# A transformer block on one core: the order of the first hundred microseconds, and the later layernorms on GpSimd

## The chip, the cores and the metric

The kernel runs as one program on one core of a Trainium2 chip. The core has five engines that each work through their own queue in order and wait for each other by semaphores: TensorE (PE, matrix products, results to PSUM), VectorE (DVE), ScalarE (ACT, activation functions), GpSimd (POOL) and SyncE (SP, which here issues all DMAs). The metric is the device time of one execution in microseconds; less is better.

## The reference

The reference is a pre-layernorm attention block followed by a gated bilinear block, both with a residual. Sequence 2048, model width 640, 32 heads of width 20, inner width 1728, everything in bfloat16:

```python
def _layernorm(x, axis=-1, eps=1e-5):
    m = jnp.mean(x, axis=axis, keepdims=True)
    v = jnp.var(x, axis=axis, keepdims=True)
    return (x - m) / jnp.sqrt(v + eps)

# attention
qkv = (x @ wqkv).reshape(B, S, 3, H, Dh).transpose(2, 0, 3, 1, 4)
scores = jnp.einsum("bhqd,bhkd->bhqk", q, k) * (Dh ** -0.5)
o = jnp.einsum("bhqk,bhkd->bhqd", softmax(scores), v)
attention = o.transpose(0, 2, 1, 3).reshape(B, S, D) @ wo
# gated bilinear block
h = (x @ w_gate) * (x @ w_up)
bilinear = h @ w_down

h  = x + attention(_layernorm(x))
h2 = h + bilinear(_layernorm(h))
```

## The kernel before

**Attention.** The 32 heads form 8 groups of four; the 2048 rows form 16 row tiles of 128 and four chunks of 512 (NB = 4, TPB = 4 row tiles in a chunk). Scores are computed transposed: for a key tile and a head, TensorE multiplies a piece of kT (32 x 128, head width padded to 32) with 512 columns of the queries. Three such products fill a PSUM tile `sc` of 128 x 1536 (three banks); there are two `sc` tiles. ScalarE takes the exponential of one in a single instruction into an SBUF tile `E` (L388); six E tiles rotate. TensorE then multiplies the E pieces with the padded V (with a column of ones, for the sums) into the one `acc` bank (AV, L474). One `sc` tile with its exponential is called a tile here, numbered from 0; there are 683. The first ones belong to the first 512 queries: for each key chunk, groups 0 to 3 in turn, five and a third tiles for each chunk and group.

**All other work is cut in between.** The eighth PSUM bank, `mi`, is a single buffer that every other product goes through: transposes of the normalised x (`job_T`, L223, five products, copied to lnT), projections to Q and K (`job_proj`, L241, five products of 512 columns, cast to qa or kT), V (`job_V`, L251, five products of 320 columns, cast to vx), and later the output projection and the bilinear block. A job cannot begin before DVE has emptied the bank of the job before it.

**The order** is written by the kernel's own planner, while it is built. `jobs` is a queue of generators that are filled in once (L584 to L627). For each tile i the main loop (L885) emits the scores and the exponential (`emit_S`), a piece of about 640 ns of the job at hand (`go_on`), AV products of earlier tiles (`emit_AV`: those up to i - 2, at most four at a time for 512 columns), and one step of the layernorms (`step_aux`). `emit_S` and `emit_AV` call `ensure` for what they need (Q, K or V), which runs the queue on until that job is done, in one go. So where a projection is not ready in the queue when its tile comes, all of it is emitted ahead of that tile's scores.

**The head.** The first chunk of x arrives in four pieces. PE does 40 products of the identity into `mi` (WARM, L518). Row tiles 0 and 1, and then 2 and 3, are normalised as pairs (`bn`, `rstd_act`, `apply1`), the square root on ACT. Each row tile is transposed (`first_T`), into `mi` for even and into `acc` for odd row tiles; ACT copies the even ones out, DVE the odd ones. `pad_half` spreads the weights to 32 columns a head: c 0, 1, 2 on ACT and 3, 4 on GpSimd for the first half of the heads, and all five on GpSimd for the second half. When all four are there, Q and K of group 0 are projected for both pairs (L553, twenty products of 256 columns, into the two `sc` tiles), ACT loads the table of Exp, and K and Q are cast by ACT and DVE.

**The later layernorms.** `gen_ln(ch)` makes the layernorm of chunks 1 to 3 in eleven steps: batch statistics of four row tiles, three steps of `rstd_steps`, and four of `apply1`. `rstd_steps` rounds mean and variance to bfloat16 and finds the square root by an integer start and three Newton steps, all on 128 x 4 values; all of this was on DVE. Chunks 2 and 3 of x are loaded into a buffer that an earlier chunk has to leave (two `xs` buffers). The steps of the second layernorms in the bilinear part use the same `rstd_steps`.

In the queue before, chunk 0 has its four V jobs and then Q and K of groups 1 to 3. A later chunk begins with its four transposes one after the other, then the load of x for two chunks later, K of group 0, V, and K of groups 1 to 3.

## Time and profile before

| | us |
|---|---|
| median of three runs | 1007.26 (1007.16 to 1008.3) |
| the profiled execution | 1010.34 |
| its span, first to last instruction | 1008.5 |
| first exponential (L388) starts | 17.92 |
| ACT busy in the span | 940.2 |
| PE busy in the span | 892.4 |
| DVE busy in the span | 322.6 |
| GpSimd busy in the span | 8.2 |
| five wp copies of GpSimd (second half of the heads) | 15.11 to 18.48 |
| load of the last chunk of x issued | 45.80 |

The span is the time between the first and the last instruction of the program, the profiled execution's time is what the device reports for it. In the profile's lines "E<-sc" is what is written and read, "x5" counts merged instructions, and a bracket holds the idle time of the engine before it and who ended it. The two numbers that begin a line of the timeline are the start and the length in microseconds. A line of the windows names the stretch, its length, the busy time of PE, PEld, DVE, ACT and POOL, the granted clock of TensorE, the DMA engines' busy share and GB/s. An engine that is busy for most of the span is not yet the bound; the chain that ended last tells which one is waited for.

### The profile page before, as it was taken

To read this page: it belongs to the slowest core of one execution; us is meant where nothing else is said; L and a number is where in the kernel's file an instruction comes from. 1 tells how busy PE (TensorE), PEld (TensorE's weight loads), DVE (VectorE), ACT (ScalarE), POOL (GpSimd) and SP (SyncE) were. 2 spreads that over 40 slices of the span, in tenths; PEclk is the share of its full clock that TensorE was granted. 3 is DMA by queue.
4 is the path that set the end of the run, shared out by engine and by line. 5 is a ranking of instruction groups with operands and counts; after the bars stand their busy time and mean duration, and the time that the engine had idled before them with its cause. 6 is when DMAs were issued, how large, how long until landed. Compare 5 with 4: busy or idle time off the path is not lost.

```text
span 1008.5 us, 17146 instructions
## 1 busy us (share of the span) xinstructions
PE 892.4 (88%) x7003; PEld 330.7 (33%) x7003; DVE 322.6 (32%) x804; ACT 940.2 (93%) x719; POOL 8.2 (1%) x62
## 2 busy tenths in 40 slices
PE   7889999999798999977798999977898999989986
PEld 4233342222132223311132333411242333434454
DVE  7783343433044322100025332110044322243232
ACT  5789999999999999999999999999999999999931
POOL 3000000000000000000000000000000000000000
PEclk8889999999587999955577999965597999979989
DMA  6000010103421320100021220000502000202210
GB/s 177 27 1 1 1 35 12 45 12 112 151 72 36 89 58 19 33 12 12 7 59 38 71 78 12 32 19 11 152 2 64 13 13 12 74 12 60 79 34 16
DMA packets 67813, 44.40 MB, mean 44 GB/s; under 512 B 18504, under 2 KB 63404, under 8 KB 67728
## 3 DMA queue, kind: packets, MB, share of 16 engines
q1 hardware_dynamic: 67728, 43.23, 15.6%
q8 instruction: 57, 0.93, 0.4%
q14 instruction: 28, 0.23, 0.1%
HBM read 35.91 MB, written 7.30 MB: 43 GB/s over the span
## 4 chain that ended last, share of the span: by engine, by line
ACT 58%; PE 22%; issue 13%; DVE 6%; DMA 1%; ACTq 0%; DVEq 0%
ACT E L388 58%; PE sc L382 5%; PE mi L730 3%; PE acc L474 3%; PE f L730 2%; PE mi L667 2%; PE mi L254 2%; PE mi L244 1%; DVE st L160 1%; PE mi L226 1%; PE f L762 1%; PE mi L762 1%; DVE kT L213 0%; PE sc L553 0%; DVE hh L737 0%
## 5 line engine op out<-in xcount | busy, mean ns | idle before, releaser
L388 ACT ACTIVATE E<-sc 128x1536 bf16<-128x1536 f32 (+1 forms) x683 | 923.1, 1715 | 21.0 <-PE sc L382 19.9
L382 PE MATMUL sc<-qa,kT 32*128 32x512 bf16 x1536 | 234.7, 446 | 70.8 <-ACT E L388 66.4
L474 PE MATMUL acc<-E,vx 128*32 128x512 bf16 (+1 forms) x2432 | 234.3, 401 | 0.0
L382 PEld LDWEIGHTS <-kT 32*128 32x128 bf16 x2432 | 97.2, 93 | 303.7 <-issue 295.9
L474 PEld LDWEIGHTS <-vx 128*32 128x32 bf16 x2432 | 57.1, 95 | 162.9 <-issue 159.8
L244 PE MATMUL mi<-lnT,wp 128*128 128x512 bf16 x310 | 89.7, 389 | 2.9 <-DVE qa L213 1.2
L382 PE MATMUL sc<-qb,kT 32*128 32x256 bf16 (+1 forms) x896 | 72.9, 304 | 10.8 <-ACT E L388 9.4
L762 PE MATMUL mi<-wd,hh 128*128 128x320 bf16 x392 | 71.1, 304 | 0.1
L213 DVE CAST u<-mi 128x512 bf16<-128x512 f32 (+3 forms) x56 | 35.0, 624 | 92.6 <-PE mi L730 92.6
L737 DVE TENSOR_TENSOR hh<-mi,u 128x512 bf16<-128x512 f32 (+3 forms) x56 | 35.0, 625 | 86.3 <-PE mi L730 86.3
L486 DVE COPY asb<-acc 128x512 f32<-128x512 f32 (+1 forms) x33 | 19.8, 600 | 120.5 <-PE acc L474 120.5
L730 PE MATMUL mi<-ln2T,wu 128*128 128x512 bf16 (+2 forms) x200 | 55.9, 384 | 1.7 <-DMA wu<-in_B_w_up_dram 0.5
L730 PE MATMUL mi<-ln2T,wg 128*128 128x512 bf16 (+2 forms) x200 | 52.8, 367 | 0.7 <-DVE u L213 0.5
L762 PEld LDWEIGHTS <-hh 128*128 128x128 bf16 x448 | 36.8, 97 | 37.1 <-issue 27.1
L667 PE MATMUL mi<-wo,on 128*128 128x320 bf16 x224 | 42.1, 313 | 0.0
L765 DVE TENSOR_TENSOR xr<-mi,h 128x320 bf16<-128x320 f32 x28 | 13.8, 492 | 88.0 <-PE mi L762 88.0
L730 PE MATMUL mi<-ln2T,qa 128*128 128x512 bf16 (+3 forms) x160 | 34.2, 328 | 1.1 <-DVE u L213 0.5
L213 DVE CAST kT<-mi 128x512 bf16<-128x512 f32 x31 | 21.3, 689 | 41.7 <-PE mi L244 41.7
L244 PEld LDWEIGHTS <-wp 128*128 128x128 bf16 x310 | 21.3, 97 | 39.6 <-issue 31.2
L670 DVE TENSOR_TENSOR h<-mi,xr 128x320 f32<-128x320 f32 x28 | 13.8, 492 | 52.0 <-PE mi L667 51.6
L254 PE MATMUL mi<-wv,lnT 128*128 128x320 bf16 x160 | 27.0, 299 | 2.9 <-DVE vx L213 2.8
L412 DVE TENSOR_TENSOR on<-asb,bc 128x512 bf16<-128x512 f32 (+1 forms) x30 | 18.2, 605 | 32.8 <-DMA bc<-scr 32.8
(115 smaller groups left out, 400.8 us busy)
## 6 DMA issues: line engine op xcount, KB each, us to landing
bc<-scr SPq DMA_DIRECT2D x100, 64.0 KB
...
```

Source lines behind the costliest of these rows:

```text
L213: nc.vector.tensor_copy(dst, src)
L244: nc.tensor.matmul(ps[:], lhsT=wslice(m, g, c), rhs=lnT[:, c, ch * QB:(ch + 1) * QB], start=(c == 0), stop=(c == KT - 1))
L254: nc.tensor.matmul(ps[:, 0:HALF], lhsT=lnT[:, c, t * P:(t + 1) * P], rhs=wv[c][:, half * HALF:(half + 1) * HALF], start=(c == 0), stop=(c ...
L382: nc.tensor.matmul(sc[:, o:o + w], lhsT=kT[g][SLOT * j:SLOT * (j + 1), kt * P:(kt + 1) * P], rhs=q_of(g, b, c0, w)[SLOT * j:SLOT * (j + 1) ...
L388: nc.scalar.activation(e[:, 0:n], sc[:, 0:n], ACT.Exp, scale=SM_SCALE)
L412: nc.vector.tensor_tensor(On[b % 2][g][:, c0:c0 + w], asb[:, 0:w], bc[:, 0:w], ALU.mult)
L474: nc.tensor.matmul(acc["t"][SLOT * j:SLOT * (j + 1), 0:w], lhsT=vx[kt][:, VS * h:VS * h + SLOT], rhs=e, start=(kt == lo), stop=(kt == hi - 1))
L486: nc.vector.tensor_copy(asb[:, 0:w], acc["t"][:, 0:w])
L667: nc.tensor.matmul(ps[:, 0:HALF], lhsT=on[g][:, t * P:(t + 1) * P], rhs=wo[g][:, cs], start=(g == 0), stop=(g == NG - 1))
L730: nc.tensor.matmul(ps[0:M, 0:n], lhsT=st["w", fp][k][:, c, f2 * P:f2 * P + M], rhs=st["ln2T"][:, c, c0:c0 + n], start=(c == 0), stop=(c == ...
L737: nc.vector.tensor_tensor(st["hh"][2 * fp + f2][0:M, c0:c0 + n], ps[0:M, 0:n], hold["u"][0:M, 0:n], ALU.mult)
L762: nc.tensor.matmul(ps[:, 0:HALF], lhsT=st["hh"][f][0:K, t * P:(t + 1) * P], rhs=late["Wd"][f][0:K, cs], start=(f == 0), stop=(f == 2 * FP ...
```

## The change

In the head, row tile 0's and 1's part of Q and K of group 0 is projected right behind their transposes (`first_proj(0)`), and the other part behind the transposes of row tiles 2 and 3. The order within is changed to alternate K and Q for each of the five slices of the width. Products of the identity that nobody reads (`keep_busy`) stand ahead of it (52 in place of 40), between the first two transposes (2), behind them (6) and behind the first projection (4).

In the queue, chunk 0 begins with Q and K of group 1, ahead of V. The transposes of the next chunk are spread over the jobs of a chunk, one behind every second V and one behind the projections of groups 2 and 3. The load of x for the chunk after next comes behind them, followed by K of group 0 of the next chunk.

The layernorms of chunks 1 to 3 go to GpSimd, except for the batch statistics and the reciprocal, which stay on DVE. GpSimd takes one more operation in each Newton step; the integer shift is merged into the next operation on both engines. For the first 48 tiles two steps of the layernorms are emitted with each tile instead of one, and the layernorm of a chunk begins when its load has been emitted. For the first 10 tiles AV stays four tiles behind rather than two.

```diff
--- before.py
+++ after.py
@@ -48,7 +48,9 @@
 END = "end"
 BUDGET = 640
 START = 440
-WARM = 40
+WARM = 52
+LAG = 10
+EARLY = 48
 
 
 @with_exitstack
@@ -160,31 +162,35 @@
             nc.vector.bn_stats(st[:, h, :], halves[h] if halves else src[:, h * HALF:(h + 1) * HALF])
         nc.vector.bn_aggr(mv[:, k, :], st[:])
 
-    def rstd_steps(mv, n):
+    def rstd_steps(mv, n, ve_=None):
+        ve_ = ve_ or nc.vector
         mb = small.tile([P, n], BF16, name="mb")
-        nc.vector.tensor_copy(mb[:], mv[:, :, 0])
+        ve_.tensor_copy(mb[:], mv[:, :, 0])
         m32 = small.tile([P, n], F32, name="m32")
-        nc.vector.tensor_copy(m32[:], mb[:])
+        ve_.tensor_copy(m32[:], mb[:])
         vb = small.tile([P, n], BF16, name="vb")
-        nc.vector.tensor_copy(vb[:], mv[:, :, 1])
+        ve_.tensor_copy(vb[:], mv[:, :, 1])
         ve = small.tile([P, n], BF16, name="ve")
-        nc.vector.tensor_scalar_add(ve[:], vb[:], EPS_B)
+        ve_.tensor_scalar_add(ve[:], vb[:], EPS_B)
         v = small.tile([P, n], F32, name="v")
-        nc.vector.tensor_copy(v[:], ve[:])
+        ve_.tensor_copy(v[:], ve[:])
         yield
         y = small.tile([P, n], F32, name="y")
-        iy = small.tile([P, n], I32, name="iy")
-        nc.vector.tensor_scalar(iy[:], v[:].bitcast(I32), 1, None, ALU.arith_shift_right)
-        nc.vector.tensor_scalar(y[:].bitcast(I32), iy[:], -1.0, float(0x5F3759DF), ALU.mult, ALU.add)
+        ve_.tensor_scalar(y[:].bitcast(I32), v[:].bitcast(I32), -0.5, float(0x5F3759DF), ALU.mult, ALU.add)
         t = small.tile([P, n], F32, name="nt")
         for k in range(3):
-            nc.vector.tensor_tensor(t[:], y[:], y[:], ALU.mult)
-            nc.vector.scalar_tensor_tensor(t[:], t[:], -0.5, v[:], ALU.mult, ALU.mult)
-            nc.vector.scalar_tensor_tensor(y[:], t[:], 1.5, y[:], ALU.add, ALU.mult)
+            ve_.tensor_tensor(t[:], y[:], y[:], ALU.mult)
+            if ve_ is nc.gpsimd:
+                ve_.tensor_tensor(t[:], t[:], v[:], ALU.mult)
+                ve_.tensor_scalar(t[:], t[:], -0.5, 1.5, ALU.mult, ALU.add)
+                ve_.tensor_tensor(y[:], t[:], y[:], ALU.mult)
+            else:
+                ve_.scalar_tensor_tensor(t[:], t[:], -0.5, v[:], ALU.mult, ALU.mult)
+                ve_.scalar_tensor_tensor(y[:], t[:], 1.5, y[:], ALU.add, ALU.mult)
             if k == 0:
                 yield
         den = small.tile([P, n], BF16, name="den")
-        nc.vector.tensor_tensor(den[:], v[:], y[:], ALU.mult)
+        ve_.tensor_tensor(den[:], v[:], y[:], ALU.mult)
         r = small.tile([P, n], F32, name="rstd")
         nc.vector.reciprocal(r[:], den[:])
         yield (m32, r)
@@ -199,10 +205,11 @@
 
     lns = {}
 
-    def apply1(t, m32, r, k):
+    def apply1(t, m32, r, k, eng=None):
+        eng = eng or nc.vector
         x_t = xs[t // TPB][:, t % TPB, :]
-        nc.vector.tensor_scalar(x_t, x_t, m32[:, k:k + 1], None, ALU.subtract)
-        nc.vector.tensor_scalar(x_t, x_t, r[:, k:k + 1], None, ALU.mult)
+        eng.tensor_scalar(x_t, x_t, m32[:, k:k + 1], None, ALU.subtract)
+        eng.tensor_scalar(x_t, x_t, r[:, k:k + 1], None, ALU.mult)
         lns[t] = x_t
 
 
@@ -513,9 +520,11 @@
         nc.vector.reciprocal(r[:], den[:])
         return m32, r
 
-    idle = mip.tile([P, BANK], F32, name="mi", tag="mi")
-    for k in range(WARM):
-        nc.tensor.matmul(idle[:, 0:P], lhsT=ident[:], rhs=ident[:], start=True, stop=True)
+    def keep_busy(n):
+        idle = mip.tile([P, BANK], F32, name="mi", tag="mi")
+        for k in range(n):
+            nc.tensor.matmul(idle[:, 0:P], lhsT=ident[:], rhs=ident[:], start=True, stop=True)
+    keep_busy(WARM)
 
     def ln_bank(k):
         if k % 2:
@@ -525,6 +534,13 @@
     pair_mv = [small.tile([P, 2, 2], F32, name="mv") for _ in range(2)]
     pK = scp.tile([P, EW], F32, name="sc")
     pQ = scp.tile([P, EW], F32, name="sc")
+    def first_proj(pr):
+        for c in range(KT):
+            for m in (1, 0):
+                nc.tensor.matmul(
+                    (pQ, pK)[m][:, pr * HW:(pr + 1) * HW], lhsT=wslice(m, 0, c),
+                    rhs=lnT[:, c, pr * HW:(pr + 1) * HW], start=(c == 0), stop=(c == KT - 1))
+
     def first_T(t, eng, after=None):
         gen = job_T(lns[t], lnT[:, :, t * P:(t + 1) * P], eng, ln_bank(t), after)
         for _ in gen:
@@ -533,26 +549,23 @@
     for k in range(2):
         bn(pair_mv[0], k, xs[0][:, k, :])
     m32, r = rstd_act(pair_mv[0], 2, lambda: bn(pair_mv[1], 0, xs[0][:, 2, :]))
-    for c in (0, 1):
+    for c in (0, 1, 3, 4):
         pad_half(c, 0)
     for k in range(2):
         apply1(k, m32, r, k)
     first_T(0, "act")
     pad_half(2, 0)
+    keep_busy(2)
     first_T(1, "dve", lambda: bn(pair_mv[1], 1, xs[0][:, 3, :]))
-    for c in (3, 4):
-        pad_half(c, 0)
+    keep_busy(6)
+    first_proj(0)
+    keep_busy(4)
     m32, r = rstd_act(pair_mv[1], 2)
     for k in range(2):
         apply1(2 + k, m32, r, k)
     first_T(2, "act")
     first_T(3, "dve")
-    for pr in range(2):
-        for m in (1, 0):
-            for c in range(KT):
-                nc.tensor.matmul(
-                    (pQ, pK)[m][:, pr * HW:(pr + 1) * HW], lhsT=wslice(m, 0, c),
-                    rhs=lnT[:, c, pr * HW:(pr + 1) * HW], start=(c == 0), stop=(c == KT - 1))
+    first_proj(1)
     nc.scalar.activation(warm[:], ones[:], ACT.Exp)
     for c in range(KT):
         pad_half(c, 1)
@@ -564,13 +577,15 @@
     def gen_ln(ch):
         ts = range(ch * TPB, (ch + 1) * TPB)
         mv = small.tile([P, TPB, 2], F32, name="mv")
+        while ch not in xs:
+            yield
         for k in range(TPB):
             bn(mv, k, xs[ch][:, k, :])
             yield
-        for got in rstd_steps(mv, TPB):
+        for got in rstd_steps(mv, TPB, nc.gpsimd):
             yield
         for k, t in enumerate(ts):
-            apply1(t, *got, k)
+            apply1(t, *got, k, nc.gpsimd)
             done.add(("a", t))
             yield
 
@@ -582,18 +597,30 @@
         aux.append(gen_ln(ch))
 
     for ch in range(NB):
-        if ch:
-            for t in range(ch * TPB, (ch + 1) * TPB):
+        nxt = deque(range((ch + 1) * TPB, (ch + 2) * TPB) if ch + 1 < NB else [])
+
+        def one_T():
+            if nxt:
+                t = nxt.popleft()
                 add(("T", t), T_of(t))
-            if ch + 2 < NB:
-                do(("x", ch + 2), lambda ch=ch: load_x(ch + 2))
-            add(("k", 0, ch), job_proj(1, 0, ch))
+        if ch == 0:
+            add(("q", 0, 1), job_proj(0, 1, 0))
+            add(("k", 1, 0), job_proj(1, 1, 0))
         for t in range(ch * TPB, (ch + 1) * TPB):
             add(("v", t, 0), job_V(t, 0))
+            if t % 2:
+                one_T()
         for g in range(1, G1):
-            if ch == 0:
+            if ch == 0 and g > 1:
                 add(("q", 0, g), job_proj(0, g, 0))
-            add(("k", g, ch), job_proj(1, g, ch))
+            if ch or g > 1:
+                add(("k", g, ch), job_proj(1, g, ch))
+            if g > 1:
+                one_T()
+        if ch + 1 < NB:
+            if ch + 3 < NB:
+                do(("x", ch + 3), lambda ch=ch: load_x(ch + 3))
+            add(("k", 0, ch + 1), job_proj(1, 0, ch + 1))
     for g in range(G1, NG):
         add(("q", 0, g), job_proj(0, g, 0))
         for ch in range(NB):
@@ -891,8 +918,10 @@
                 ensure(("spill", g))
             load_res()
         used = go_on(BUDGET)
-        emit_AV(i - 2 if i < n_tiles else i)
+        emit_AV(i if i >= n_tiles else i - 2 if i >= LAG else i - 4)
         step_aux()
+        if i < EARLY:
+            step_aux()
         run_events(i)
         if b_seen < NB - 1 and normed(str(b_seen), range(NG)):
             add_tail(b_seen, list(range(TPB)))
```

## The prediction

> **What bounds the kernel now.** I read the page first: busy shares, the slices and the chain that ended last.
>
> ```profile
> PE 892.4 (88%) x7003; PEld 330.7 (33%) x7003; DVE 322.6 (32%) x804; ACT 940.2 (93%) x719; POOL 8.2 (1%) x62
> ...
> PEclk8889999999587999955577999965597999979989
> ...
> ACT 58%; PE 22%; issue 13%; DVE 6%; DMA 1%; ACTq 0%; DVEq 0%
> ```
>
> ACT is busy for 93% of the span and carries the chain: the 683 exps of L388, 1.33 us from one to the next, set the time. The change touches only the first hundred microseconds, so the second view is the busy time of each engine by stretch, cut at the first exp (17.92), at the end of the last gap of the head (74.45) and at the last exp.
>
> ```profile
> 0.00:17.92 17.92, 11.30 (x84) 8.88 (x85) 11.59 (x38) 7.33 (x12) 7.65 (x62) 0.81 0.84 241
> 17.92:74.45 56.53, 48.70 (x332) 16.98 (x332) 44.76 (x145) 47.47 (x35) 0.56 (x1) 0.88 0.05 15
> 74.45:959.40 884.95, 796.50 (x6313) 278.67 (x6312) 250.50 (x575) 874.50 (x648) 0.00 (x0) 0.87 0.16 43
> ```
>
> The columns are PE, PEld, DVE, ACT and POOL busy, then the granted clock. ACT idles 9.1 us between 17.92 and 74.45 and only 10.5 us in the 885 us behind. What the head wins or loses in exp starts moves the end by as much. Third, the timeline of ACT alone, where the bracket is the idle time before an exp:
>
> ```profile
> 28.09 6.89 ACT L388 ACTIVATE E<-sc 128x1536 bf16<-128x1536 f32 x5 [3.25 <-PE sc L382]
> ...
> 42.97 1.45 ACT L388 ACTIVATE E<-sc 128x1536 bf16<-128x1536 f32 x1 [0.84 <-PE sc L382]
> ...
> 48.90 4.52 ACT L388 ACTIVATE E<-sc 128x1536 bf16<-128x1536 f32 x3 [1.03 <-PE sc L382]
> ...
> 68.48 1.45 ACT L388 ACTIVATE E<-sc 128x1536 bf16<-128x1536 f32 x1 [1.05 <-PE sc L382]
> ...
> 74.45 6.86 ACT L388 ACTIVATE E<-sc 128x1536 bf16<-128x1536 f32 x5 [1.04 <-PE sc L382]
> ```
>
> With the smaller ones of that view (0.33, 0.26, 0.28, 0.23, 0.29, 0.29) the gaps sum to 8.9 us. Their causes, in the timeline of all engines: Q and K of group 1 are forced before tile 5, one after the other through the single mi bank,
>
> ```profile
> 23.54 1.25 PE L244 MATMUL mi<-lnT,wp 128*128 128x512 bf16 x5
> ...
> 25.57 1.24 PE L244 MATMUL mi<-lnT,wp 128*128 128x512 bf16 x5 [0.78 <-DVE qa L213]
> 26.85 0.69 DVE L213 CAST kT<-mi 128x512 bf16<-128x512 f32 x1 [1.33 <-PE mi L244]
> ```
>
> (4.55 us from 23.54 to the exp at 28.09), and the bunched transposes leave PE idle 1.9 us, after which its clock is halved for 6.8 us:
>
> ```profile
> 40.28:43.69 3.41, 1.29 (x16) 0.76 (x16) 3.27 (x13) 2.57 (x3) 0.00 (x0) 1.00 0.02 5
> 43.69:47.10 3.41, 3.41 (x25) 1.09 (x23) 2.25 (x12) 2.87 (x3) 0.00 (x0) 0.50 0.12 8
> ```
>
> PE busy 1.29 of 3.41 us, then clock 0.50. The same happened in 64.17 to 67.58 (1.41 busy) and in 6.14 to 9.56 (0.91).
>
> **The change, part by part.** X is the start of the first exp, X8 that of exp 8, and so on, counted from 0. Stretches on PE, from the timeline at full clock: scores of a tile (S) 0.32, its AV products 0.33, three products of 512 0.75, five transposes 0.4; at half clock (44 to 50) 0.54, 0.54, 1.40 and 0.64. A V (five products of 320) is 0.79, at half an estimated 1.45 by the products of 512.
>
> First exp. Twelve more warming products at 0.11 us end at 7.1, under the first transposes at 7.59: nothing. The two products behind them write the mi bank that ACT reads until 8.77, so the second transposes start at 9.0 instead of 8.31; DVE is in batch statistics until 9.3 anyway, and its copy slips from 9.21 to 9.5. All that follows on DVE slips 0.3: third and fourth transposes ready at 11.5 and 12.2 (before 11.19, 11.91). Projection needs the copies to 9.95; 20 products took 4.29 at half clock, so ten take 2.15, or 1.07 at full. At full clock all is hidden, the last copy ends at 13.25, the other ten products at 14.3, and as Q's end led the exp by 1.21, X is 15.5: 2.4 gained. At half clock the first ten end at 12.2, four idle products at 12.6, two transposes of 0.72 at 14.05, the copy at 14.65, ten products at 16.8: X is 18.0, 0.1 lost. I take the middle, 1.2 gained. The Exp table load (1.28) still ends before K's copy.
>
> The old gaps go: 8.9 us gained. Tiles 0 to 3 carry group 1's Q and K in pieces (S 0.32, three products 0.75: under 1.33).
>
> What comes instead is on DVE's queue. The later layernorms' small instructions go to GpSimd, but the reciprocal stays on DVE, in the middle of its order, and DVE waits there until GpSimd has done eighteen instructions, all but one of which wait for the one before. Rows for GpSimd:
>
> ```profile
> 0.75 0.20 POOL masks.py:197 MEMSET ident<- 128x128 bf16 x1 [0.29 <-POOLq L990]
> 1.02 0.29 POOL masks.py:199 TENSOR_SCALAR_AFFINE_SELECT ident<-ident 128x128 bf16<-128x128 bf16 x1
> ...
> L154 POOL COPY wp<-wo 128x640 bf16<-128x640 bf16 x5 | 3.4, 720 | 5.6 <-DMA wo<-in_A_wqkv_dram 5.6
> ```
>
> From 0.29 at 128 elements and 0.72 at 640 the slope is 0.84 ns, so 4 elements cost an estimated 0.19; the select started 0.07 after what it waits for. That is 0.26 each, 4.6 us the chain. Bounds: the one-column memset (0.10) plus 0.07 gives 3.1; the whole select plus 0.07 gives 6.5. I take 4.6, since the operations read as the copy does. DVE's cost was 0.20 each. The Trainium skill speaks against this part: "GPSIMD Engine Reference", section "Key points", holds VectorE structurally about 2x faster for elementwise work. By that the chain would be 18 x 0.40 = 7.2 us, and the sum 7.8 us higher; no row here shows it. GpSimd's five wp copies ahead of the chain end at 18.5: free. The applies (0.72 each by the copy row) have the transposes late enough to hide them.
>
> A, first layernorm. DVE runs two statistics (1.03 each: two halves of 0.88 together and the merge), Q1's cast at X+1.6, two statistics: done X+4.2. Chain to X+8.9, reciprocal, V0's cast at X+9.0 to 9.5, although V0's products were done at X+5.3. AV and V1 wait for it, and tile 6's scores stand behind both: 0.1+0.33+0.79+0.39+0.1 at full clock, 0.1+0.54+1.45+0.54+0.1 at half. Exp 6 comes at X+11.2 to 12.2, due at X+8.0: lost 3.2 to 4.2; I take 3.9, as 3.7 us of idle PE should halve the clock.
>
> B, tiles 6 and 7 hold one transpose and two V in one bank: AV, transposes, a statistic in the way (1.0), copy 0.46, V2, cast 0.49, AV, V3, S: 5.0 us at full, 7.0 at half, less two exps (2.7): 2.3 to 4.3; I take 3.3.
>
> C, second layernorm: its statistics end about 1.8 us before X8, the chain at X8+2.9, then the copy of the transposes of tile 5, X8+3.6. Only then group 2's Q and K, forced together before tile 10 as group 1's were before tile 5: 4.55 us, or 6.8 at half clock. Exp 10 at X8+8.2 to 10.4, due X8+2.7: 5.5 to 7.7; I take 6.6.
>
> D, third layernorm. Its x can be fetched only when the transposes of row tile 7 (in tile 15, about X15) have read the buffer. Nothing stands before it on SP. The old fetch:
>
> ```profile
> 45.80 0.37 SPq L120 DMA_DIRECT2D xs<-in_A_x_dram  x1
> ...
> 49.00:50.00 1.00, 1.00 (x5) 0.10 (x3) 0.27 (x2) 1.00 (x1) 0.00 (x0) 0.50 0.35 126
> 50.00:51.00 1.00, 1.00 (x10) 0.36 (x8) 0.96 (x3) 0.94 (x2) 0.00 (x0) 0.74 0.00 0
> ```
>
> The DMA share falls to nothing at 50, so 4.3 us. Two steps a tile put the four statistics in DVE's queue right away, ahead of V4's cast: 4.3 + 4.1 + 0.5, then V5 and tile 20's scores (1.2 to 2.0) and 0.3 of handovers. Exp 20 at X15+10.4 to 11.2, due X15+6.7: 3.7 to 4.5; I take 4.2.
>
> E, its chain ends about X20+2.1, ahead of the copy of row tile 8: exp 22 at X20+4.0 to 4.8, due 2.7; with the tile after it I take 2.5 (1.3 to 3.5). G, tiles at half clock cost 0.26 to 0.29 each in the old gaps; five: 1.4 (0 to 2).
>
> The other edits cost nothing: AV two tiles later fits the six E buffers, the shift merged into the multiply saves 0.2 us on an idle DVE, and the order behind the head is the old one.
>
> Sum: 3.9+3.3+6.6+4.2+2.5+1.4 = 21.9 lost, 8.9+1.2 gained: 11.8 slower. The profiled execution took 1010.34 (span 1008.5), so 1022.1; its 3.1 above the median is the same on both sides, so 1019.1 for the runs.
>
> The other rule concerns the clock. Rows: 1.9 us of idle halved it. "TensorE: Matmul & The Clock Gate", section "HAM oscillation", only warns of idle gaps over about 3.4 us; by it B, C, D and G would go at full clock: 1.0, 1.1, 0.5 and 1.4 less, 1015.1.
>
> **The rivals.** Slow GpSimd (0.36 a step): three chains 1.9 longer, 5.7 more: 1024.8; with every part at its half-clock end another 4.3: 1029. For: two-input operations have no row. Against: the copy's small fixed part.
>
> Fast chain and full clock: 0.17 a step takes 1.5 from each of A, C, E, full clock 4.0 from B, C, D, G: 3.3 slower, 1010.6. For: with chains of 3.1 PE idles less. Against: in A it still idles 2.2 us, more than the 1.9 that halved the clock.
>
> Faster: if dependent instructions followed each other as the memsets of vx do (48 in 2.5 us, 0.05 each), a chain takes 0.9 us. The point is V0 in A: 1.1 us lie between the last statistic and V0's end, 0.06 a step. Below it A and E are gone, PE does not idle, B loses its statistic in the way (1.3 left), C costs what the forced pair cost before (3.3), D 3.7, G 0, and the first exp gains 2.4: 8.3 lost against 11.3, 3.0 faster, 1004.3. Against: those memsets depend on nothing; the one dependent pair took 0.27.
>
> The idle products hold no clock: the first exp stays at 18.0, 1020.4, within the main case.
>
> **How the numbers follow.** Main case, 12 us slower give or take 4: 0.62 (1015 to 1024). Slow GpSimd: 0.16. Fast chain at full clock: 0.15. Faster: 0.05; a balance within 0.2% (2 us, what a measurement can tell): 0.02. Slower is 0.93. The range takes the fast chain's 1010.6 and the slow one's 1029, leaving the faster side out.
>
> **What would show it.** Right: in the timeline of DVE, idle time of about 3 us ahead of the reciprocal (L195 of the new kernel), released by GpSimd's den; ACT gaps before exps 6, 8, 10 and 20 of 3 to 8 us; none before exp 5; half clock between 24 and 50. A first exp after 18 or before 15.5 breaks that step. No idle before the reciprocals, or GpSimd steps under 0.1, would make the forecast wrong; so would group 2's pair no longer starving ACT.

## The result, and the profile after

The changed kernel takes 1031.57 us (median of four runs, 1028.56 to 1033.71), the kernel before beside it 1007.78 (1007.16 to 1008.85): ratio 1.0226, 95% interval 1.0210 to 1.0241. It is 23.8 us slower, twice the 11.8 that were forecast. The profiled execution took 1031.6, its span is 1029.6 (before 1008.5, so 21.1 more). Three lines of its page answer to those of before:

```profile
PE 892.0 (87%) x6974; PEld 336.3 (33%) x7027; DVE 306.4 (30%) x722; ACT 938.8 (91%) x719; POOL 64.2 (6%) x143
...
PEclk9689999999868899975558899975587999989989
...
ACT 57%; PE 22%; issue 12%; DVE 4%; POOL 3%; DMA 1%; ACTq 0%; POOLq 0%; SPq 0%; DVEq 0%
```

GpSimd works 64.2 us in place of 8.2 and DVE only 16.2 less: the same layernorms cost GpSimd three and a half times what they cost DVE. GpSimd is now in the chain that ended last. The busy time by stretch (PE, PEld, DVE, ACT, POOL, then granted clock), cut at the first exp, at the last gap of the head and at the last exp:

```profile
0.00:16.72 16.72, 12.26 (x107) 10.40 (x109) 12.17 (x38) 7.23 (x13) 7.33 (x61) 0.90 0.86 248
16.72:84.85 68.13, 42.21 (x252) 14.90 (x254) 25.98 (x64) 36.15 (x26) 50.60 (x80) 0.77 0.05 15
84.85:981.00 896.15, 801.98 (x6346) 284.90 (x6392) 252.49 (x574) 884.39 (x657) 6.27 (x4) 0.87 0.15 42
```

Between 16.72 and 84.85 ACT idles 32.0 us (before 9.1 in the stretch of the head's gaps), and behind 84.85 it idles 11.8 in 896 us, much as before. So the loss lies in the head. ACT's own timeline says where; exps are counted from 0, the first line holds exps 0 to 5:

```profile
16.72 8.16 ACT L395 ACTIVATE E<-sc 128x1536 bf16<-128x1536 f32 x6 [0.70 <-PE sc L389]
29.39 1.45 ACT L395 ACTIVATE E<-sc 128x1536 bf16<-128x1536 f32 x1 [4.51 <-PE sc L389]
...
34.74 2.79 ACT L395 ACTIVATE E<-sc 128x1536 bf16<-128x1536 f32 x2 [2.20 <-PE sc L389]
54.01 1.45 ACT L395 ACTIVATE E<-sc 128x1536 bf16<-128x1536 f32 x1 [16.48 <-PE sc L389]
...
73.28 2.79 ACT L395 ACTIVATE E<-sc 128x1536 bf16<-128x1536 f32 x2 [3.81 <-PE sc L389]
77.83 1.45 ACT L395 ACTIVATE E<-sc 128x1536 bf16<-128x1536 f32 x1 [1.76 <-PE sc L389]
```

The gap ahead of exp 5 is gone. New gaps stand ahead of exps 6, 8, 10, 20 and 22, which are the forecast's terms A, B, C, D and E. With the small ones the gaps of the first 100 us sum to 31.97, before to 8.89; less the 1.20 of the earlier first exp that is 21.9, against 21.1 in the span. All but C sum to 15.5, where the forecast had 15.3. C alone is 16.48, where it had 6.6.

What C waits for is read backwards. The scores ahead of exp 10 stand behind the projections of Q and K of group 2, which are emitted together there (the forced pair), and these waited for DVE:

```profile
47.16 0.59 PE L251 MATMUL mi<-lnT,wp 128*128 128x512 bf16 x1 [11.17 <-DVE lnT L220]
```

DVE's timeline (the bracket is the idle time before, and who ended it):

```profile
20.96 0.64 DVE L220 CAST kT<-mi 128x512 bf16<-128x512 f32 x1
26.19 0.18 DVE L195 RECIPROCAL rstd<-den 128x4 f32<-128x4 bf16 x1 [4.59 <-POOL den L193]
26.29 0.46 DVE L220 CAST vx<-mi 128x320 bf16<-128x320 f32 x1
...
33.90 0.21 DVE L163 BATCH_NORM_AGGREGATE mv<-st 128x2 f32<-128x12 f32 x1
34.35 0.49 DVE L220 CAST vx<-mi 128x320 bf16<-128x320 f32 x1 [0.24 <-PE mi L261]
46.55 0.18 DVE L195 RECIPROCAL rstd<-den 128x4 f32<-128x4 bf16 x1 [11.70 <-POOL den L193]
46.65 0.46 DVE L220 COPY lnT<-mi 128x640 bf16<-128x640 bf16 x1
```

Twice DVE stands at the reciprocal of the layernorm, with the cast or copy of the one `mi` bank behind it. The first wait is the chain of dependent steps, as forecast (nineteen of them in the trace, where the forecast counted eighteen). The second is 11.70, and GpSimd's timeline shows what GpSimd did meanwhile:

```profile
26.13 1.89 POOL L211 TENSOR_SCALAR xs<-xs,m 128x640 bf16<-128x640 bf16 x1
28.12 1.89 POOL L212 TENSOR_SCALAR xs<-xs,rstd 128x640 bf16<-128x640 bf16 x1
...
39.65 1.89 POOL L212 TENSOR_SCALAR xs<-xs,rstd 128x640 bf16<-128x640 bf16 x1
41.48 0.19 POOL L168 CAST mb<-mv 128x4 bf16<-128x4 f32 x1
...
46.32 0.20 POOL L193 TENSOR_TENSOR den<-v,y 128x4 bf16<-128x4 f32 x1
```

The second layernorm's statistics were ready at 34.1, but its chain began at 41.48, behind eight applies of the first layernorm at 1.89 each. The forecast had 0.72 for one of them, from the row of a copy of the same size. The chain itself took 5.05 (forecast 4.6).

### The profile page after: what moved, and what is told of

Same layout as the page of the kernel before. It is cut to its first block, busy times and chain, and to the rows that moved or that the text cites. A ratio compares the mean times of both kernels' runs of the same rounds, so it can differ in the third digit from the quotient of the medians.

```text
span 1029.6 us, 17140 instructions
## 1 busy us (share of the span) xinstructions
PE 892.0 (87%) x6974; PEld 336.3 (33%) x7027; DVE 306.4 (30%) x722; ACT 938.8 (91%) x719; POOL 64.2 (6%) x143
## 4 chain that ended last, share of the span: by engine, by line
ACT 57%; PE 22%; issue 12%; DVE 4%; POOL 3%; DMA 1%; ACTq 0%; POOLq 0%; SPq 0%; DVEq 0%
ACT E L395 57%; PE sc L389 5%; PE acc L481 3%; PE mi L757 3%; PE mi L251 3%; PE f L757 2%; PE mi L694 2%; PE mi L261 2%; DVE st L162 1%; PE mi L233 1%; PE f L789 1%; POOL xs L212 1%; POOL xs L211 1%; DMA xs<-in_A_x_dram 1%; DMA wg<-in_B_w_gate_dram 1%
## 5 line engine op out<-in xcount | busy, mean ns | idle before, releaser
L389 PEld LDWEIGHTS <-kT 32*128 32x128 bf16 x2432 | 99.8, 93 | 297.9 <-issue 285.9
L251 PE MATMUL mi<-lnT,wp 128*128 128x512 bf16 x287 | 87.2, 393 | 16.8 <-DVE lnT L220 11.7
L757 PE MATMUL mi<-ln2T,wu 128*128 128x512 bf16 (+2 forms) x186 | 53.7, 382 | 2.7 <-DMA wu<-in_B_w_up_dram 0.7
L251 PEld LDWEIGHTS <-wp 128*128 128x128 bf16 x310 | 22.8, 99 | 52.2 <-issue 44.5
L757 PE MATMUL mi<-ln2T,qa 128*128 128x256 bf16 (+3 forms) x153 | 33.9, 326 | 1.5 <-DVE u L220 0.5
L220 DVE CAST qa<-mi 128x512 bf16<-128x512 f32 x23 | 15.9, 691 | 38.7 <-PE mi L251 38.7
```

The source lines that it names most:

```text
L220: nc.vector.tensor_copy(dst, src)
L251: nc.tensor.matmul(ps[:], lhsT=wslice(m, g, c), rhs=lnT[:, c, ch * QB:(ch + 1) * QB], start=(c == 0), stop=(c == KT - 1))
L389: nc.tensor.matmul(sc[:, o:o + w], lhsT=kT[g][SLOT * j:SLOT * (j + 1), kt * P:(kt + 1) * P], rhs=q_of(g, b, c0, w)[SLOT * j:SLOT * (j + 1) ...
L757: nc.tensor.matmul(ps[0:M, 0:n], lhsT=st["w", fp][k][:, c, f2 * P:f2 * P + M], rhs=st["ln2T"][:, c, c0:c0 + n], start=(c == 0), stop=(c == ...
```

## The experiments

Four theories. **Queue**: the second chain stands behind the slow applies in GpSimd's order, DVE's reciprocal waits for it, and the casts behind that wait too. **Chain**: the nineteen dependent steps on GpSimd (the expectations say eighteen) are the cost, wherever the applies end. **Pace**: two layernorm steps a tile put the layernorms in front of the casts that feed ACT, on whichever engine they run. **Order**: the new order of jobs is too much for PE and DVE at any pace. Some expectations name a fifth, **apply**: applies of 1.89 are late for the transposes by themselves.

All runs in one table; all versions hold the changed head. "Steps" are layernorm steps a tile in the first 48 tiles; in the columns of the chain and the applies D is DVE and P GpSimd. "Gaps" are ACT's idle times between exps in the first 100 us of the profiled execution (8.89 before). "Against before" is the ratio less 1, times 1008.4 (its medians in these comparisons were 1007.8 to 1009.2).

| version | order | steps | chain | applies | gaps | ratio (95%) | against before |
|---|---|---|---|---|---|---|---|
| e5_head_only | old | 1 | D | D | 7.1 | 0.9957 (0.9941 to 0.9974) | -4.3 |
| e12_pace_only | old | 2 | D | D | 17.8 | 1.0057 (1.0033 to 1.0080) | +5.7 |
| e7_dve_early0 | new | 1 | D | D | 12.2 | 1.0014 (0.9993 to 1.0034) | +1.4 |
| e3_all_dve | new | 2 | D | D | 24.7 | 1.0159 (1.0135 to 1.0182) | +16.0 |
| e2_chain_dve | new | 2 | D | P | 23.0 | 1.0122 (1.0105 to 1.0139) | +12.3 |
| e1_apply_dve | new | 2 | P | D | 29.5 | 1.0211 (1.0194 to 1.0228) | +21.3 |
| changed kernel | new | 2 | P | P | 32.0 | 1.0226 (1.0210 to 1.0241) | +22.8 |
| e10_fused | new | 2 | P | P, one each | 29.6 | 1.0155 (1.0137 to 1.0173) | +15.6 |
| e19_cheap_apply | new | 2 | P | P, cheap form | 25.9 | 1.0163 (1.0145 to 1.0181) | +16.4 |
| e8_after_early0 | new | 1 | P | P | 19.5 | 1.0120 (1.0095 to 1.0145) | +12.1 |
| e4_old_order_pool | old | 1 | P | P | 12.5 | 1.0018 (1.0003 to 1.0033) | +1.8 |
| e22_old_pool_cheap | old | 1 | P | P, cheap form | 4.9 | 0.9962 (0.9949 to 0.9975) | -3.8 |
| e16_old_apply_pool | old | 1 | D | P | 8.6 | 0.9989 (0.9977 to 1.0002) | -1.1 |
| e20_old_cheap | old | 1 | D | P, cheap form | 6.2 | 0.9958 (0.9943 to 0.9974) | -4.2 |
| e11_mixed | old | 1 | P | half D, half P | 8.5 | 0.9982 (0.9967 to 0.9998) | -1.8 |
| e13_qk_first | part | 1 | D | D | 10.1 | 0.9989 (0.9974 to 1.0003) | -1.1 |
| e14_qk_first_apply_pool | part | 1 | D | P | 7.1 | 0.9976 (0.9964 to 0.9988) | -2.4 |

The intervals of e7, e13 and e16 hold 1, so these three are not told apart from before. Where a version has a few long runs, the difference of the medians is lower than the ratio says: 0.1 faster for e7, 0.5 slower for e4, 2.7 faster for e13.

### Parts undone

**All later layernorms on DVE.**

```diff
-        for got in rstd_steps(mv, TPB, nc.gpsimd):
+        for got in rstd_steps(mv, TPB):
...
-            apply1(t, *got, k, nc.gpsimd)
+            apply1(t, *got, k)
```

> The changed kernel with the later layernorms all on DVE again, chain and applies; head, order of the queue, two steps a tile and AV two tiles later stay. Queue theory and chain theory: what GpSimd cost goes, gaps A (exp 6), C (exp 10) and E (exp 22) with it; the forced pair (3.3) and the load of the third chunk (D, 3.7) stay as before's gaps did, and the time is 1004 to 1009 (3 faster to 2 slower than before). Pace theory: with two steps a tile the layernorm's 25 to 30 us of DVE work are packed in front of the casts that the projections wait for, on whichever engine; gaps of 1.4 (exp 5), 4 (exp 6), 2 to 4 (exp 8), 6 to 7 (exp 10), 4.6 (exp 20) and 2 (exp 22) remain, and the time is 13 to 16 us above before (1020 to 1023). Then GpSimd added only some 8 to 10 of the 23.8.

16.0 slower: pace or order, not GpSimd. GpSimd added only 6.8 of the 22.8. ACT's timeline of this version:

```profile
29.71 1.45 ACT L395 ACTIVATE E<-sc 128x1536 bf16<-128x1536 f32 x1 [3.99 <-PE sc L389]
...
36.83 2.79 ACT L395 ACTIVATE E<-sc 128x1536 bf16<-128x1536 f32 x2 [3.81 <-PE sc L389]
46.24 1.45 ACT L395 ACTIVATE E<-sc 128x1536 bf16<-128x1536 f32 x1 [6.62 <-PE sc L389]
...
65.28 1.45 ACT L395 ACTIVATE E<-sc 128x1536 bf16<-128x1536 f32 x1 [3.77 <-PE sc L389]
```

These are A, B, C and D, nearly at the sizes that the forecast gave them, without anything on GpSimd. All engines around A:

```profile
23.00 0.84 PE L261 MATMUL mi<-wv,lnT 128*128 128x320 bf16 x5 [2.08 <-DVE kT L220]
...
24.24 0.18 DVE L195 RECIPROCAL rstd<-den 128x4 f32<-128x4 bf16 x1
...
24.33 0.36 DVE L211 TENSOR_SCALAR xs<-xs,m 128x640 bf16<-128x640 bf16 x1
...
26.16 0.39 DVE L212 TENSOR_SCALAR xs<-xs,rstd 128x640 bf16<-128x640 bf16 x1
26.46 0.48 DVE L220 CAST vx<-mi 128x320 bf16<-128x320 f32 x1
```

V0's products are done at 23.84, its cast comes at 26.46. In the changed kernel it came at 26.29. What GpSimd takes off DVE ahead of that cast (chain and three row tiles of applies) DVE now spends waiting for GpSimd's chain.

**The head alone.** The layernorms go back to DVE as above, and the queue's part of the change is undone.

```diff
-LAG = 10
-EARLY = 48
+LAG = 0
+EARLY = 0
...
-        nxt = deque(range((ch + 1) * TPB, (ch + 2) * TPB) if ch + 1 < NB else [])
...
+        if ch:
+            for t in range(ch * TPB, (ch + 1) * TPB):
                 add(("T", t), T_of(t))
...
-        if ch == 0:
-            add(("q", 0, 1), job_proj(0, 1, 0))
-            add(("k", 1, 0), job_proj(1, 1, 0))
...
```

> The changed kernel's head alone (first pair projected between the transposes, idle products); layernorms on DVE, order, steps a tile and AV's distance as before. All theories: the first exponential at 16.7 (17.92 before) as in the changed kernel, the old gaps as before, and 1.2 us faster than before (0.5 to 1.8). A time equal to before would say that the 1.2 of the head is given back by the old gaps, which hang on the loads and on GpSimd's wp copies and not on the first exponential.

4.3 faster, outside the 0.5 to 1.8 expected. In its profiled execution the first exp is 1.56 earlier (16.36) and the gaps 1.8 smaller; the spans differ by 5.3, and the other 1.9 is not located.

**The old order with the layernorms on GpSimd.** The queue's part alone is undone.

> The changed kernel's head and its layernorms on GpSimd (chain and applies), but the queue's order, the one layernorm step a tile and AV's distance as before. Chain theory: each of three chains puts its 5 us ahead of a cast, about 10 us slower than before (1014 to 1020). Queue theory: in the old order a chunk's transposes come 16 tiles (21 us) apart, longer than the 15 us of applies and the 5 us chain, so the chains seldom meet the applies; a balance between old gaps kept (8.9) and one new gap of some 4.5 us where the third chunk's transposes are forced: 0 to 4 above before. Pace theory: the old order is what matters, not more than 3 above before.

1.8 slower (0.5 by the medians): the chain theory falls. But against the head alone GpSimd costs 6.1 here as well, and again by its queue. The third chain begins at 62.37, as the second chunk's last apply ends, and the reciprocal at 67.44 has 5.75 us of DVE's idle time ahead of it, then the gap of 5.00 ahead of exp 31.

### Pace and order

**One step a tile in the version with all on DVE**, and **two steps a tile in the head alone**:

```diff
-EARLY = 48
+EARLY = 0
```

```diff
-EARLY = 0
+EARLY = 48
```

> The changed kernel with the later layernorms on DVE and one layernorm step a tile in place of two in the first 48 tiles; head, order of the queue and AV's distance stay. With two steps this kernel was 16.0 above before, the head alone 4.3 below it, so 20 us are shared by the order and by the pace. Pace theory (two steps a tile put four statistics and the chain ahead of the casts, 4.1 us and 3.6 us in one piece): the gaps ahead of exps 6, 10, 20 and 22 shrink to 1, 3.5, 0.5 and 0, and the time is 2 below to 3 above before. Order theory (the jobs of the first 20 tiles are simply more than PE and DVE can do beside the exponentials, at any pace): the gaps move but their sum of 23 stays, 12 to 17 above before.

> The head alone, with two layernorm steps a tile in the first 48 tiles; layernorms on DVE, order of the queue and AV's distance as before. The head alone was 4.3 below before. Pace theory: the statistics now stand ahead of V's and Q's casts in tiles 1 to 5 (four gaps of 1.2 to 1.5), and the third layernorm ahead of exp 21 waits for its load (5 us): 1 to 6 above before. Order theory: the pace by itself does nothing in the old order, 3 to 5 below before, as the head alone.

Both came out as the pace theory said: the second step costs 14.6 us in the new order (16.0 less 1.4) and 10.0 in the old (5.7 and 4.3). What remains for the order with AV's distance is 5.7 (1.4 and 4.3; 4.2 by the medians). At one step a tile V0's cast is at 22.29, and the reciprocal at 25.83, behind V1's cast: the layernorm's steps now stand behind the casts that they stood ahead of.

**The changed kernel with one step a tile** (the first of the two diffs above, on the changed kernel):

> The changed kernel with one layernorm step a tile in place of two; chain and applies on GpSimd, order and head stay. Queue theory with the pace: the second chunk's chain is given to GpSimd six tiles later and finds the applies done, so the gap of 16.5 ahead of exp 10 falls to about 4; the first chain still stands ahead of V's cast (gap of 6 to 7 at exp 7 in place of 4.5 at exp 6), and the third chain's applies make a gap of about 4.5 ahead of exp 30 in place of 3.8 and 1.8 ahead of exps 20 and 22: 10 to 14 above before. Chain theory: the chain costs the same wherever it stands, 20 to 24 above before.

12.1 slower, where the queue theory had 10 to 14: gaps of 6.79 ahead of exp 7, 3.28, 3.40 and 5.40 ahead of exps 8, 10 and 30. (Its profiled execution is the fastest of its four, 1014.90; the median is 1019.45.)

### GpSimd's part

**One apply in place of two**: subtraction and multiplication in one instruction, with no rounding in between.

```diff
-        eng.tensor_scalar(x_t, x_t, m32[:, k:k + 1], None, ALU.subtract)
-        eng.tensor_scalar(x_t, x_t, r[:, k:k + 1], None, ALU.mult)
+            eng.tensor_scalar(x_t, x_t, m32[:, k:k + 1], r[:, k:k + 1], ALU.subtract, ALU.mult)
```

> The changed kernel with one edit: each apply on GpSimd is one instruction (subtract and multiply together) in place of two, so GpSimd has four applies a chunk and not eight. The rounding to bfloat16 between the two is left out. Measured so far: an apply instruction takes 1.89 us on GpSimd, eight of them stand between the first layernorm's chain and the second's, and the changed kernel is 23.8 us slower than before, 16.5 us of which is the one gap of ACT ahead of exp 10. Queue theory (the second chain stands behind the applies in GpSimd's order, DVE's reciprocal waits for it, and what is behind the reciprocal waits too): four instructions of 1.9 go, 7.5 us earlier, the gap ahead of exp 10 falls from 16.5 to about 9, and the time is about 16 us above before (14 to 18). Chain theory (the eighteen dependent steps are the cost, wherever the applies end): gap and time stay, 23 to 24 us above before. Pace theory (the new order of the queue with two layernorm steps a tile starves ACT, GpSimd only shares in it): gap ahead of exp 10 falls to no less than the 6 to 7 that the order alone would make, and then any time between 14 and 24 is left open by it.

15.6 slower, in the queue theory's range. The gap ahead of exp 10 fell to 11.25 and not to 9, because the fused instruction takes 2.50: four of them are 5.1 shorter than eight of 1.89, and the gap is 5.2 smaller.

**Only the applies back on DVE**, and **only the chain back on DVE**:

```diff
-            apply1(t, *got, k, nc.gpsimd)
+            apply1(t, *got, k)
```

```diff
-        for got in rstd_steps(mv, TPB, nc.gpsimd):
+        for got in rstd_steps(mv, TPB):
```

> The changed kernel with the applies back on DVE; the chain stays on GpSimd, and so do order, head and two steps a tile. Queue theory (the second chain was late because it stood behind eight applies of 1.89 on GpSimd): the chain starts as soon as its statistics are done, the gap ahead of exp 10 falls from 16.5 to 7 to 8; in exchange three applies of 0.77 now stand behind the first reciprocal, ahead of V's first cast, so the gap ahead of exp 6 grows from 4.5 to 6.7: 17 to 20 above before. Chain theory (eighteen dependent steps on GpSimd are the cost by themselves): 22 to 24 above before, as the changed kernel. If neither part of GpSimd's work costs anything alone, it is the time of the version with all on DVE, 16.

> The changed kernel with the chain back on DVE; the applies stay on GpSimd, and so do order, head and two steps a tile. Queue theory: nothing that DVE waits for stands behind the applies any more except the transposes; DVE is free of 0.77 for each row tile, so it is better than all on DVE (16.0 above before): gaps of 2 ahead of exp 6, 3.4 ahead of exp 8, 4.5 ahead of exp 10, 9 to 12 above before. Apply theory (GpSimd's applies at five times DVE's price are late for the transposes themselves): 16 to 24 above before.

The first: gaps of 6.77 and 8.05 ahead of exps 6 and 10, as the queue theory had them, but 21.3 in all, between the two ranges, with 3.96 ahead of exp 22. The second: 12.3, close above the queue theory's range, with 8.23 ahead of exp 10 where 4.5 was expected; what makes up the rest is not shown. So against all on DVE the chain alone costs 5.3, the applies alone gain 3.7, and both together cost 6.8: the 5.2 beyond their sum fits the chain behind the applies, which needs both on GpSimd. With intervals of about 1.7 either way for each time, the signs hold, the last digits do not.

### The price of an apply

**Instructions that nobody needs, on a GpSimd that has nothing else to do**, in the head alone, on the tiles `wo[0]` (b, bfloat16) and `wo[1]` (f, read as float32), which are free at that time:

```diff
+        g.tensor_scalar(b[:], b[:], one[:], None, ALU.mult)
+        g.tensor_scalar(b[:], b[:], 0.5, None, ALU.mult)
+        g.tensor_scalar(b[:], b[:], one[:], one[:], ALU.mult, ALU.mult)
+        g.tensor_scalar(b[:, 0:HALF], b[:, 0:HALF], one[:], None, ALU.mult)
+        g.tensor_scalar(b[:, 0:P], b[:, 0:P], one[:], None, ALU.mult)
+        g.tensor_tensor(b[:], b[:], b[:], ALU.mult)
...
+        g.tensor_scalar(f[:], f[:], one[:], None, ALU.mult)
...
```

> The head alone (all layernorms on DVE) with fourteen GpSimd instructions that nobody needs, one after the other on tiles that are free at that time: the apply's form alone. If the per-partition scalar makes it 1.89, the same with a constant takes 0.7 to 0.9; if it is arithmetic on bfloat16, both take 1.89 and the form with float32 is shorter by element; if it is the loop over elements, 320 elements take about 1.04 and 128 about 0.53 (0.19 at 4 elements and 2.66 ns an element), whatever the type, and the two-operation form 1.9 as in the fused run. The rival, that the apply was long because it shared something with DVE's or PE's work beside it: 0.7 to 1.0 here. The time is the head's own, 4 below before, give or take 2.

GpSimd's timeline, in the order of the diff:

```profile
19.31 1.89 POOL L607 TENSOR_SCALAR wo<-wo,pone 128x640 bf16<-128x640 bf16 x1
21.28 1.81 POOL L608 TENSOR_SCALAR wo<-wo 128x640 bf16<-128x640 bf16 x1
23.20 0.88 POOL L609 TENSOR_SCALAR wo<-wo,pone 128x640 bf16<-128x640 bf16 x1
24.17 1.08 POOL L610 TENSOR_SCALAR wo<-wo,pone 128x320 bf16<-128x320 bf16 x1
25.34 0.61 POOL L611 TENSOR_SCALAR wo<-wo,pone 128x128 bf16<-128x128 bf16 x1
26.04 1.25 POOL L612 TENSOR_TENSOR wo<-wo 128x640 bf16<-128x640 bf16 x1
...
28.45 1.09 POOL L615 TENSOR_SCALAR wo<-wo,pone 128x320 f32<-128x320 f32 x1
```

It is 1.89 here as well; a constant saves 0.08; float32 costs the same by element; 2.5 ns an element from 128 to 640 (1.28 us in 512). The odd line is L609: two multiplications in one instruction take less than half of one. (The single run took 1004.10, as the head alone.)

This run does not rule out contention: DVE worked all through the two long instructions (L607, L608) and stood idle during the short one (L609). The changed kernel rules it out: its applies from 35.81 to 41.5 ran while DVE stood idle (34.85 to 46.55, above), the last two with PE and ACT idle too, and took 1.89 each like those beside DVE's work. In the next run the short forms stay short beside a busy DVE.

It is DVE that pays. The same step of the chain on DVE, in the version with the applies on GpSimd (e2; an apply had begun there at 34.92) and with all on DVE (e3):

```profile
35.00 0.73 DVE L179 TENSOR_SCALAR y<-v 128x4 int32<-128x4 int32 x1
```

```profile
21.59 0.17 DVE L179 TENSOR_SCALAR y<-v 128x4 int32<-128x4 int32 x1
```

In the next run a DVE apply took up to 0.85 beside GpSimd's instructions, where it takes 0.38. In the changed kernel no DVE instruction between the first exp and 100 us is longer than in the versions with all on DVE by as much as 0.1, so this is no part of its loss. Where applies on GpSimd meet chain steps or applies on DVE it costs DVE 1.4 to 2.7 us in that stretch (e2, e11, e14, e16, e20).

**Which pairs are cheap**: nine more forms in the same place.

```diff
+        g.tensor_scalar(b[:], b[:], one[:], one[:], ALU.mult, ALU.mult)
+        g.tensor_scalar(b[:], b[:], one[:], 1.0, ALU.mult, ALU.mult)
+        g.tensor_scalar(b[:], b[:], 1.0, one[:], ALU.mult, ALU.subtract)
+        g.tensor_scalar(b[:], b[:], one[:], one[:], ALU.mult, ALU.subtract)
+        g.tensor_scalar(b[:], b[:], one[:], one[:], ALU.mult, ALU.add)
+        g.tensor_scalar(b[:], b[:], one[:], 1.0, ALU.subtract, ALU.mult)
+        g.tensor_scalar(b[:], b[:], one[:], one[:], ALU.add, ALU.mult)
+        g.tensor_scalar(b[:], b[:], one[:], None, ALU.subtract)
+        g.tensor_scalar(b[:], b[:], one[:], None, ALU.add)
```

> The head alone (all layernorms on DVE) with nine GpSimd instructions that nobody needs, all on 128 x 640 bfloat16 in place. If an instruction with two operations is cheap whatever they are, and a lone one dear: 0.9 for all seven with two, 1.9 for lone subtract and add; but then the fused apply of the earlier run (2.50) does not fit. If only multiply is cheap as first operation and anything may follow: 0.9 for multiply-multiply (also with a constant), multiply-subtract and multiply-add, 2.5 for subtract-multiply and add-multiply. If only multiply-multiply is cheap: 0.9 for two of them, 2.5 for the others.

```profile
18.85 0.88 POOL L607 TENSOR_SCALAR wo<-wo,pone 128x640 bf16<-128x640 bf16 x1
19.82 0.80 POOL L608 TENSOR_SCALAR wo<-wo,pone 128x640 bf16<-128x640 bf16 x1
20.73 2.44 POOL L609 TENSOR_SCALAR wo<-wo,pone 128x640 bf16<-128x640 bf16 x1
23.29 2.50 POOL L610 TENSOR_SCALAR wo<-wo,pone 128x640 bf16<-128x640 bf16 x1
25.88 0.89 POOL L611 TENSOR_SCALAR wo<-wo,pone 128x640 bf16<-128x640 bf16 x1
26.87 2.43 POOL L612 TENSOR_SCALAR wo<-wo,pone 128x640 bf16<-128x640 bf16 x1
29.40 0.88 POOL L613 TENSOR_SCALAR wo<-wo,pone 128x640 bf16<-128x640 bf16 x1
30.38 1.89 POOL L614 TENSOR_SCALAR wo<-wo,pone 128x640 bf16<-128x640 bf16 x1
32.36 1.89 POOL L615 TENSOR_SCALAR wo<-wo,pone 128x640 bf16<-128x640 bf16 x1
```

None of the three guesses: pairs of multiplications and additions take 0.80 to 0.89, a pair with a subtraction 2.43 to 2.50, a lone operation 1.89, subtraction or addition. Why, these runs do not show. (The single run took 1009.68, beside a single run of 1009.46 before.)

The Trainium skill, "GPSIMD Engine Reference", section "Engine selection", holds GpSimd about 2 times slower than VectorE for two inputs and roughly at line rate for one. Here the applies, which read one tensor, took 0.38 and 0.39 on DVE: the cheap form is 2.1 times that, the lone form 4.9 times. In the chain, which is elementwise too, a step takes 0.20 on GpSimd where DVE takes 0.16, and follows the one before after 0.28 where DVE does after 0.20. There the measurement decides against a factor of 2.

**The changed kernel with the cheap form**, both roundings kept; the mean is negated where it was copied before (`neg` is set for the later layernorms):

```diff
+        if neg:
+            ve_.tensor_scalar(m32[:], mb[:], -1.0, 1.0, ALU.mult, ALU.mult)
...
-        eng.tensor_scalar(x_t, x_t, m32[:, k:k + 1], None, ALU.subtract)
-        eng.tensor_scalar(x_t, x_t, r[:, k:k + 1], None, ALU.mult)
+            eng.tensor_scalar(x_t, x_t, m32[:, k:k + 1], 1.0, ALU.add, ALU.mult)
+            eng.tensor_scalar(x_t, x_t, r[:, k:k + 1], 1.0, ALU.mult, ALU.mult)
```

> The changed kernel with the applies on GpSimd in a form of 0.8 to 0.9 in place of 1.89: adding the negated mean (negated where it was copied before) and multiplying by one, then multiplying by the reciprocal and by one. Both roundings stay, no instruction is added. Queue theory with the forecast's sum: the second chain's way is free at 0.85 as it was forecast at 0.72; the gap ahead of exp 10 falls from 16.5 to 6.5 to 8, the others stay at 4.5, 2 to 4, 3.8 and 1.8; 13 to 16 above before. Apply theory falls if it does so; if the gap stays over 12, the price was not the cause. Chain theory: 20 to 24 above before.

Its applies take 0.80, and it is 16.4 slower, just above the 13 to 16 expected. Its ACT and DVE:

```profile
46.76 1.45 ACT L402 ACTIVATE E<-sc 128x1536 bf16<-128x1536 f32 x1 [9.21 <-PE sc L396]
```

```profile
39.30 0.18 DVE L198 RECIPROCAL rstd<-den 128x4 f32<-128x4 bf16 x1 [4.44 <-POOL den L196]
```

C falls from 16.48 to 9.21, where 6.5 to 8 was expected; under 12, so the price was a cause of it. The second chain now begins at 34.19, as its statistics end. The price of the apply was worth 6.4 us of the time, give or take 2.4. All the layernorms on GpSimd at this price come out 0.4 above all on DVE, which is no difference that can be told.

### Towards a better version

**Old order, chain on GpSimd, applies shared** (odd row tiles of a chunk on GpSimd, on top of the old order):

```diff
-            apply1(t, *got, k, nc.gpsimd)
+            apply1(t, *got, k, nc.gpsimd if k % 2 else None)
```

> A version meant to beat both: the head alone (old order, one step a tile), with the chain of the later layernorms on GpSimd and their applies shared, row tiles 1 and 3 of a chunk on GpSimd, 0 and 2 on DVE. With all applies on GpSimd this order was 1.8 above before, with a gap of 5.0 ahead of exp 31 where the third chunk's forced transposes wait for eight applies of 1.89; with all layernorms on DVE (the head alone) 4.3 below. Queue theory: four applies of 1.89 beside four of 0.38 end early enough, the gap ahead of exp 31 falls to 1 to 1.5, DVE is relieved: 5 to 8 below before. Chain theory: three chains of 5 us stay, 1 to 3 above before.

1.8 faster, between the two ranges, although the gap ahead of exp 31 is 1.47 as the queue theory had it. Applies on DVE beside applies on GpSimd took 0.64 to 0.82 in six cases where they take 0.38; that is 2.3 us of DVE's time, and how much of the missing gain it explains is not shown.

**Of the new order only Q and K of group 1 ahead of V** (and AV's distance), and **the same with the applies on GpSimd**:

```diff
+        if ch == 0:
+            add(("q", 0, 1), job_proj(0, 1, 0))
+            add(("k", 1, 0), job_proj(1, 1, 0))
...
```

```diff
-            apply1(t, *got, k)
+            apply1(t, *got, k, nc.gpsimd)
```

> The head, AV's distance and, of the new order, only Q and K of group 1 ahead of V; the transposes stay in one piece at the start of a chunk, the load and K of group 0 behind them, one layernorm step a tile, layernorms on DVE. The whole new order at one step a tile was 1.4 above before, the head alone 4.3 below. If the spread transposes are what the order costs (they put four more fillings of the one bank into tiles 6 to 10, and pull the second layernorm forward): 3 to 8 below before. If Q and K ahead of V costs it (V and the forced pair of group 2 come later): 0 to 3 above before.

> The version with Q and K of group 1 first, transposes in one piece and one step a tile, with the applies of the later layernorms on GpSimd and the chain on DVE. Queue theory: in this order the applies have 10 us and more until the transposes and no chain stands behind them, DVE is free of 9.2 us: 1 to 4 faster than the same with all on DVE. Apply theory: eight applies of 1.89 are late for transposes in one piece, a gap of 4 or more in tiles 15 to 31 and slower than the same with all on DVE.

1.1 and 2.4 faster than before. The first lies between its two guesses: some 3.2 of the order's 5.7 is Q and K ahead of V, 2.5 the spread transposes, with intervals that leave the shares open. The second is 1.3 below the first by the ratios and 0.4 above it by the medians: these runs do not tell them apart.

**Old order with only the applies on GpSimd, at 1.89 and in the cheap form, and with chain and cheap applies:** (the diffs above on the head alone)

> The head alone, with only the applies of the later layernorms on GpSimd; order, one step a tile, chain on DVE as before. Queue theory: 15 us of applies end before the forced transposes, 21 us later; DVE is free of 9.2 us; no chain waits: 4 to 7 below before, as the head alone (4.3) or a little better. Apply theory (1.89 each is late for the transposes by itself): a gap of 3 to 5 ahead of exp 16 or 31, and 2 below to 2 above before.

> The head alone with only the applies on GpSimd, in the form of 0.8 to 0.9; chain on DVE, order and one step a tile as before. With applies of 1.89 it was 1.1 below before, the head alone 4.3 below. If the long applies were late for the transposes there (gaps of 1.0 to 1.5 ahead of exps 15, 18 and 31): 4 to 7 below before. If GpSimd's work slows DVE beside it (casts and copies longer than alone) or the difference is one of the clock's windows: 0 to 3 below before.

> The head alone with chain and applies on GpSimd, the applies in the form of 0.8 to 0.9; order and one step a tile as before. With applies of 1.89 it was 1.8 above before. Queue theory: the gap of 5.0 ahead of exp 31 goes to 0.5 to 1, DVE is free of 20 us: 4 to 8 below before. Chain theory: the chain keeps costing, 0 to 2 above before.

1.1, 4.2 and 3.8 faster. At 1.89 gaps of 1.0 to 1.5 remain ahead of exps 15, 17, 18 and 31, in the tiles of the transposes; at 0.80 those there are 0.8 or less. In the old order with chain and applies on GpSimd the price alone is worth 5.6 (1.8 and -3.8). None of them beats the head alone (4.3 faster); it and the two with cheap applies beat both kernels: the layernorms on GpSimd add nothing that can be measured to the head.

## Why the prediction was wrong

**The step that failed: "The applies (0.72 each by the copy row) have the transposes late enough to hide them."** They take 1.89, and the cover named was the wrong one. What came late was not the transposes but the next layernorm's chain, in the same queue: fifteen us of applies stood in front of it. Term C was 6.6 and measured 16.48. With applies of 0.80 it is 9.21. Of the 11.0 by which the ratio's 22.8 exceeds the forecast, 6.4 go with the price. The row that the price came from is a copy; no row of the kernel before shows a subtraction or multiplication by a scalar on GpSimd.

**Term C was also short at the right price** by 2.6. The statistics ended 0.65 ahead of X8 and not 1.8, the chain took 5.05 and not 4.6 (it has nineteen instructions, and the sum counted eighteen), and the forced pair ran at half clock throughout (0.50 granted from 37.4 to 51.0 in the run with the cheap form); with these the forecast's own upper end, X8+10.4, becomes 12.0, which is what was measured (34.76 to 46.76). Beside A to E the changed kernel has three gaps, where the forecast had G, five tiles at half clock (1.4): 0.25, 0.28 and, ahead of exp 12, 1.42. The last is longer than G's 0.26 to 0.29 a tile and had no term.

**Right in size, but not for the cause named alone: A and E, and C as forecast.** A came out at 4.51 (3.9), E at 1.76, or 3.0 with the tiles behind it (2.5). In the trace of the changed kernel they are what the forecast said, a wait for GpSimd's chain. But with all on DVE the same steps leave 3.99 (A), 6.62 (C, forecast 6.6) and 1.90 (E), so that the sizes fit is in part luck: the two steps a tile had the layernorm stand ahead of the same casts on DVE. The forecast spoke of the pace only in D; by the table, the 22.8 are -4.3 for the head, 5.7 for the order, 14.6 for the pace and 6.8 for GpSimd, added in this order. In another order the shares differ: with GpSimd already in, the pace is 10.7 (22.8 and 12.1). The rival "Faster" failed by the same: in it A and E go with the chain's price, and without any chain on GpSimd they stay.

**Right: D, and nearly B.** D is 3.81 (4.2), and DVE's first statistic waits 0.85 for the load issued at 62.35; with all on DVE it is 3.77. B is 2.20, just under its bounds (3.3, bounds 2.3 to 4.3). The gap ahead of exp 5 went, dependent steps of the chain were 0.28 apart (0.26).

**The first exp: 16.72, as forecast to the digit, by luck.** The forecast took the middle between full and half clock all through; in the changed kernel the clock was halved for one stretch, from 9.92 to 13.34, and full again for the second ten products. In the nineteen executions profiled with this head the clock was halved for one stretch between 8.5 and 13.7 in eight, and the first exp came at 16.33 to 17.04; in eleven it was not, and it came at 15.55 to 16.20. The rival "idle products hold no clock" describes the eight, though never as late as its 18.0.

**The rivals.** "Slow GpSimd" priced the chain's steps, which were right, at 1024.8 to 1029; nothing in it was slow applies. The fast chain and the factor of 2 for the chain did not come. The signs of the list came true: idle time of DVE ahead of the reciprocals, gaps ahead of exps 6, 8, 10 and 20, none ahead of exp 5, half clock in the stretch forecast (27.0 to 30.4 and 37.2 to 57.7); but of the gaps 2.2 and 16.5 lay outside "3 to 8".
